# Two sliding-attention/FFN layers on one core: the order of the first layer norms, and one more tile's statistics on ScalarE

## Chip, cores, metric

One core of a Trainium2 chip. The metric is the device time of one execution in microseconds (us), as the median of the runs. A core has five engines that run side by side and meet through semaphores: PE (TensorE: matmuls and transposes into PSUM), DVE (VectorE), ACT (ScalarE), POOL (GpSimd) and SP (SyncE, which here only issues DMAs).

## What is computed

The input x has 2048 tokens of 1024 features in bf16. Two layers are applied, each of an attention block and a feed-forward block, with the same weights in both layers:

```python
x = x + A(layernorm(x), wqkv, wo)      # sliding attention, 32 heads of 32
x = x + B(layernorm(x), w1, b1, w2, b2) # 1024 -> 3584, gelu, -> 1024
# A: q, k, v = x @ wqkv; each position looks at 8 positions, 2 apart, at and before its own:
#    softmax over the 8 logits, weighted sum of v, then @ wo
# layernorm: (x - mean) / sqrt(var + 1e-5), no scale or offset
```

## The kernel before

All of x stays on the chip as 16 tiles `x[0]` to `x[15]` of 128 tokens. Four tiles make a group of 512 tokens; layer by layer and group by group the work items are n = 0 to 7. An item goes through `gen_qkv` (queries, keys and values in 8 chunks each, a chunk being 8 matmuls of 512 columns over the 8 slices k of the features), the attention proper on DVE (products of queries and keys, softmax, products with the values), `gen_wo` (output projection), `gen_ffn1` and `gen_ffn2`. Weights are loaded again for every item in tiles `wt` of 1 MB or 896 KB, in five buffers. PSUM is used as eight accumulators `acc` in rotation. The driver at the end of the program interleaves these parts: `stage` runs one of them unit by unit and calls `sides` at stated units, so attention on DVE for one item goes on beside PE's matmuls for another.

The wrapper `InOrder` records each engine's instructions. While its `on` is set, every instruction is tied to stand behind the last one of that engine in program order; `hold` makes everything later stand behind the last one. Where neither is set, the compiler's scheduler chooses. At the start of the program DVE, ACT, POOL and SP are all in order, and so is PE always.

**The start (`ln_first`, `queries_of_raw`).** PE can't wait until the first group is normalised. For tiles 0 and 1 it transposes the raw x (the function `transpose_on_pe`, two PSUM banks; ACT copies the banks to `raw` in two parts, the first two slices and then the other six, `copy_transposed`). Matmuls of seven query chunks c run over the raw x, slice by slice: `row(c, k)` for k = 0 to 7. Mean and inverse standard deviation enter afterwards: they are transposed on PE into rows (`spread_stats`, at (k, c) = (2, 6)), and `finish(c)` applies them, one DVE and one POOL instruction per chunk. Tiles 2 and 3 are normalised on DVE (`rest`) and transposed on PE within the same loop, at (5, 3) and (7, 6), both into the tile `bank`, which ACT copies to `xnT`. The eighth chunk follows in one piece (`row(7, k)`, `finish(7)`).

For keys and values the normalised tiles 0 and 1 are needed too. DVE writes them to `xn01`, and SP transposes them by DMA to `xnT` (list `first_early`). The order in which SP issues is:

```python
for xn, out in first_early:                        # two transposing DMAs, tiles 0 and 1
    sp.dma_start_transpose(out, xn.rearrange("s (k p) -> s k p", p=P))
wk = load_qkv(1, lambda: load_x(1, 2, 3))          # key weights: half, x[6], half
load_x(1, 3, 4)                                    # x[7]
load_x(2)                                          # x[8] to x[11]
early_tiles = ln_early((1, None), (2, qk_next))
```

**The next two groups (`ln_early`, `ln_stats_ahead`, `ln_end`).** The eight tiles of groups 1 and 2 are normalised during item 0. A tile takes two `bn_stats` (half a tile each) and a `bn_aggr` on DVE, a square root on ACT, a reciprocal and a `tensor_scalar` (the normalisation) on DVE, and a transposing DMA from SP. `ln_early` does tiles 4 to 9 one after the other, with the statistics of the next tile ahead of the normalisation of this one; it is a generator, and after its first step `last()`, which is `finish(7)`, is called. After the second step SP issues the loads of the value weights `wv`. For tiles 10 and 11 `ln_stats_ahead` takes the sums on ACT instead (Identity and Square, each with an accumulated sum) and mean and inverse root on POOL, at unit 9 of the stage; `ln_end` normalises and transposes them at unit 11.

In the lines of the profile, L92 is the line in `InOrder` through which every instruction of DVE, ACT, POOL and SP passes, L117 is the matmul helper `mm`, L230 the transposes of `transpose_on_pe`, L293 those of `spread_stats`. So groups are told apart by the names of their tiles: `stats`, `mvs` and `stds` are the layer norm's, `big` is a pool of three large buffers used for products and for normalised tiles, `vT` in the first 16 us is `raw`.

Of the kernel before, what the change touches and what calls it, by code (L numbers as in the profile page):

```python
# [8 lines left out]
ACT = mybir.ActivationFunctionType  # L9
# [8 lines left out]
def kernel(  # L18
# [18 lines left out]
    P = 128  # L37
# [195 lines left out]
    def copy_transposed(out, bank, parts):  # L233
        pst = bank[:].bitcast(BF16).rearrange("p (k t) -> p k t", t=P)
        for k0, k1 in zip(parts[:-1], parts[1:]):
            act.copy(out[:, k0:k1, :], pst[:, k0:k1, :])
# [11 lines left out]
    def ln_first():  # L248

        xnT = xa[0] = new_xnT()  # L250
        vec.on = act.on = True
        raw = attp.tile([P, KD, NT + 2], BF16, name="vT", bufs=2)
        vec.memset(raw[:, :, NT:NT + 2], 1.0)
        mv = lnp.tile([P, 4, 2], F32, name="mvs", bufs=1)
        std = lnp.tile([P, 4], F32, name="stds", bufs=1)
        rstd = lnp.tile([P, 4], F32, name="rstds", bufs=1)
        less = lnp.tile([P, 2], F32, name="lesses", bufs=1)

        def stats(tt):
            st6 = lnp.tile([P, 2, 6], F32, name="stats")  # L260
            for h in range(2):
                vec.bn_stats(st6[:, h, :], x[tt][:, h * HALF:(h + 1) * HALF])
            vec.bn_aggr(mv[:, tt, :], st6[:])

        def root(tt):
            act.activation(std[:, tt:tt + 1], mv[:, tt, 1:2], ACT.Sqrt, bias=eps_t[:])

        def norm(tt, out):
            if tt > 1:
                vec.reciprocal(rstd[:, tt:tt + 1], std[:, tt:tt + 1])  # L270
            vec.tensor_scalar(out=out, in0=x[tt][:], scalar1=mv[:, tt, 0:1], scalar2=rstd[:, tt:tt + 1],
                              op0=ALU.subtract, op1=ALU.mult)
            return out

        warm_ps = acc_tile()
        warm_up(7, warm_ps)
        banks = [acc_tile(), acc_tile()]
        for tt in range(2):
            transpose_on_pe(x[tt], raw[:, :, tt * P:(tt + 1) * P], banks[tt], (0, 2))
        warm_up(2, warm_ps)  # L280
        stats(0)
        root(0)
        copy_transposed(raw[:, :, 0:P], banks[0], (2, KD))
        stats(1)
        root(1)
        copy_transposed(raw[:, :, P:NT], banks[1], (2, KD))
        vec.tensor_scalar(out=less[:], in0=mv[:, 0:2, 0], scalar1=-1.0, scalar2=None, op0=ALU.mult)
        vec.reciprocal(rstd[:, 0:2], std[:, 0:2])
        by_token = iop.tile([P, 4, P], F32, name="tmp")

        def spread_stats(bank):
            for i, column in enumerate((less[:, 0:1], less[:, 1:2], rstd[:, 0:1], rstd[:, 1:2])):
                pe(nc.tensor.transpose(bank[:, i * P:(i + 1) * P], column.to_broadcast([P, P]), identf[:]))  # L293
            rows = by_token[:].rearrange("p i t -> p (i t)")
            act.copy(rows, bank[:])
            return rows[:, 0:NT], rows[:, NT:2 * NT]

        xn01 = bigp.tile([P, 2, D], BF16, name="big")
        first_early.append((norm(0, xn01[:, 0, :]), xnT[:, 0, :, :]))

        def rest():
            for tt in range(2, 4):
                stats(tt)
                root(tt)
                if tt == 2:
                    first_early.append((norm(1, xn01[:, 1, :]), xnT[:, 1, :, :]))
                xn = lnp.tile([P, D], BF16, name="xn", bufs=3)
                norm(tt, xn[:])
                first_late.append((xn, xnT[:, tt, :, :]))

        return raw, spread_stats, rest

    def queries_of_raw(wq, qT):
        raw, spread_stats, rest = st.pop("raw")
        first = {}

        def row(c, k):
            if k == 0:
                first[c] = acc_tile()
            mm(first[c][:, 0:NT + 2], lhsT=wq[k // (KD // 2)][:, k % (KD // 2), c::NCH], rhs=raw[:, k, :],  # L320
               start=(k == 0), stop=(k == KD - 1), skip_group_check=True)

        part = attp.tile([P, NCH, NT], F32, name="abc")

        def finish(c):
            vec.scalar_tensor_tensor(out=part[:, c, :], in0=less, scalar=first[c][:, NT:NT + 1], in1=first[c][:, 0:NT],
                                     op0=ALU.mult, op1=ALU.add)
            pool.tensor_tensor(out=qT[:, c, 0:NT], in0=part[:, c, :], in1=rstd, op=ALU.mult)

        for k in range(KD):  # L330
            for c in range(7):
                row(c, k)
                if (k, c) == (0, 6):
                    bank = acc_tile()
                if (k, c) == (2, 6):
                    less, rstd = spread_stats(bank)
                    rest()
                if (k, c) == (5, 3):
                    transpose_on_pe(*first_late.pop(0), bank)
                if (k, c) == (7, 6):  # L340
                    transpose_on_pe(*first_late.pop(0), bank, (0, KD // 2, KD))
        act.on = False
        act.hold()
        for c in range(7):
            finish(c)
        for k in range(KD):
            row(7, k)
        vec.on = False
        return lambda: finish(7)
# [41 lines left out]
    def gen_qkv(n, defer=False, qk_pool=None, v_late=False, qk_next=None, v_first=False, mix=0):  # L391
# [29 lines left out]
        if n == 0:  # L421
            last = queries_of_raw(wq, qT)
            for xn, out in first_early:
                sp.dma_start_transpose(out, xn.rearrange("s (k p) -> s k p", p=P))
            wk = load_qkv(1, lambda: load_x(1, 2, 3))
            load_x(1, 3, 4)
            load_x(2)
            early_tiles = ln_early((1, None), (2, qk_next))
            for tt in range(2):
                next(early_tiles)  # L430
                if tt == 0:
                    last()
            wv = load_qkv(2)
            for _ in early_tiles:
                pass
            vec.hold()
            sp.on = False
            sp.hold()
# [212 lines left out]
    def ln_early(*groups):  # L651

        tiles = []
        for n, pool in groups:
            xa[n] = new_xnT(pool)
            xns = bigp.tile([P, NTT, D], BF16, name="big") if pool is None else pool.tile([P, NTT, D], BF16, name="qT")
            for tt in range(NTT):
                xn = lnp.tile([P, D], BF16, name="xn", bufs=3)[:] if pool is None and tt > 1 else xns[:, tt, :]
                tiles.append((n * NTT + tt, xn, xa[n][:, tt, :, :]))
        vec.on = True  # L660
        ahead = ln_stats(tiles[0][0], root=True)
        on_act = tiles[-2:]
        tiles = tiles[:-2]
        for i, (t, xn, xT) in enumerate(tiles):
            mv_rstd = ahead
            if i + 1 < len(tiles):
                ahead = ln_stats(tiles[i + 1][0], root=True)
            vec.reciprocal(mv_rstd[1][:], mv_rstd[1][:])
            ln_norm(t, *mv_rstd, xn)
            sp.dma_start_transpose(xT, xn.rearrange("s (k p) -> s k p", p=P))  # L670
            if i + 1 == len(tiles):
                vec.on = False
            yield
        ln_rest.append(on_act)

    ln_rest = []

    def ln_end():
        vec.on = True
        for tt, (t, xn, xT) in zip((NTT - 2, NTT - 1), ln_rest.pop()):  # L680
            ln_norm(t, mv_ahead[:, tt, :], rstd_ahead[:, tt, :], xn)
            sp.dma_start_transpose(xT, xn.rearrange("s (k p) -> s k p", p=P))
        vec.on = False
# [27 lines left out]
    with tc.tile_pool(name="early", bufs=1) as early:  # L711
        sp.on = True
        load_x(1, 0, 2)
        stage(gen_qkv(0, qk_next=early), sides=at(9, ln_stats_ahead, 2, NTT - 2) + at(14, pool.dma_start, mask[0::NTT, :, :], first[:]) + at(11, ln_end) + at(14, load_b2))
        q1 = gen_qkv(1, defer=True, qk_pool=early, mix=NCH // 2)
        stage(q1, sides=at(0, gather, 0) + at(11, between, 0, 1) + at(11, hold) + each(av, 0, 12, 1))
        q2 = gen_qkv(2, defer=True)
        stage(q2, 18, sides=each(lambda n, q: load_b1(q), 2, 4, 4, 0, 4))
        hold()
        stage(gen_wo(0))  # L720
        hold()
        stage(q2, sides=at(0, new_prod, 1, 3, False) + at(0, add_prods, 1) + each(new_prod, 1, 0, 1, 4, 8))
        gather(1)
# [51 lines left out]
```

## Time and profile before

| | |
|---|---|
| median of 4 runs | 1229.05 us (1229.0 to 1229.18) |
| profiled execution | 1229.15 us, of which the span of the instructions is 1227.4 us |
| TensorE clock granted | 1.0 |
| busy in the span | PE 1222.7, DVE 865.8, ACT 314.8, POOL 121.7 us |
| DMA | 227 MB, mean 185 GB/s; from 16 to 22 us 394 GB/s |

A line of a timeline reads: start, length, engine, line of the program, operation, output<-input with shapes, count, and in brackets the idle time before it with what ended that. Neighbouring instructions of one kind are merged into one line. "SPq" is SP's instruction that issues a DMA; its length is the issuing, not the transfer. A line of waits reads: who waited for whom, us in total, times, longest. A line of DMA issues ends with KB each and the us from issue to landing. A group of instructions ends with the count, the busy time, the mean of one in ns and the idle time before.

### The profile page before, as it was taken

How to read it: one execution, taken by the hardware profiler on the slowest of the kernel's cores; microseconds unless marked ns; L12 is line 12 of the kernel's file. 1: busy time of each engine (PE TensorE's matmuls, PEld its weight loads, DVE VectorE, ACT ScalarE, POOL GpSimd, SP SyncE). 2: the span in 40 equal slices, each digit the busy share in tenths (PEclk: the TensorE clock that was granted, in tenths of full speed). 3: DMA queues.
4: the chain of work that ended last, by engine and by line, in shares of the span. 5: the costliest groups of instructions: out<-in, count | busy, mean ns of one | idle time of the engine just before them, and what ended most of it. 6: DMA issues, size and time to landing. Idle time of an engine off the chain costs nothing.

```text
span 1227.4 us, 14025 instructions
## 1 busy us (share of the span) xinstructions
PE 1222.7 (100%) x5769; PEld 632.1 (52%) x5769; DVE 865.8 (71%) x926; ACT 314.8 (26%) x498; POOL 121.7 (10%) x217
## 2 busy tenths in 40 slices
PE   9999999999999999999999999999999999999998
PEld 7666544456444554446544465444654444444444
DVE  7999897998997999375993759937598797011001
ACT  4443253014410244102431024310234001300310
POOL 2430006010101101100001000000000001000000
PEclk9999999999999999999999999999999999999999
DMA  9976665765738645856557565586664558446441
GB/s 312 263 233 181 182 201 170 202 186 191 226 120 257 183 151 162 237 172 172 168 158 223 172 171 187 153 217 199 171 204 148 186 191 211 149 160 193 158 135 51
DMA packets 225824, 227.18 MB, mean 185 GB/s; under 512 B 74000, under 2 KB 192928, under 8 KB 223712
## 3 DMA queue, kind: packets, MB, share of 16 engines
q1 hardware_dynamic: 216304, 208.17, 56.3%
q0 software_dynamic: 8880, 17.07, 4.3%
q8 instruction: 45, 0.74, 0.3%
q10 hardware_dynamic: 576, 1.05, 0.2%
q14 instruction: 19, 0.16, 0.0%
HBM read 189.01 MB, written 4.19 MB: 157 GB/s over the span
## 4 chain that ended last, share of the span: by engine, by line
PE 99%; DMA 0%; DVE 0%; ACT 0%; issue 0%
PE acc L117 99%; DMA x<-in_A_x_dram 0%; DVE stats L92 0%; PE acc L230 0%; ACT vT L92 0%; PE acc L293 0%; DVE mvs L92 0%; DVE x L92 0%; ACT stds L92 0%
## 5 line engine op out<-in xcount | busy, mean ns | idle before, releaser
L117 PE MATMUL acc<-xnT,wt 128*128 128x512 bf16 (+1 forms) x3328 | 712.9, 377 | 0.0
L117 PEld LDWEIGHTS <-wt 128*128 128x128 bf16 x3392 | 400.7, 119 | 318.8 <-issue 0.9
L117 PE MATMUL acc<-wt,hT 128*128 128x512 bf16 (+1 forms) x1820 | 388.1, 376 | 0.0
L117 PEld LDWEIGHTS <-hT 128*128 128x128 bf16 x1820 | 178.1, 98 | 209.0
L92 DVE TENSOR_TENSOR big<-big 128x2048 bf16<-128x2048 bf16 (+2 forms) x185 | 244.9, 1352 | 2.2
L92 ACT ACTIVATE hT<-acc,b1T 128x512 bf16<-128x512 f32 x224 | 151.7, 689 | 322.9 <-PE acc L117 322.8
L92 DVE TENSOR_TENSOR big<-qT,kT 128x4096 bf16<-128x4096 bf16 x64 | 143.8, 2283 | 37.7 <-ACT kT L92 35.9
L92 DVE TENSOR_TENSOR big<-abc,vT 128x4096 bf16<-128x4096 bf16 x64 | 144.6, 2283 | 8.3 <-DMA abc<-a 6.6
L92 DVE TENSOR_TENSOR tmp<-acc,b2bc 128x512 f32<-128x512 f32 x56 | 38.6, 689 | 156.1 <-PE acc L117 153.0
L92 ACT CAST qT<-acc 128x512 bf16<-128x512 f32 (+1 forms) x64 | 35.5, 558 | 278.1 <-PE acc L117 276.7
L117 PE MATMUL acc<-wt,oT 128*128 128x512 bf16 x448 | 97.9, 379 | 0.0
L92 DVE BATCH_NORM_STATS2 stats<-x 128x6 f32<-128x512 bf16 x116 | 77.3, 680 | 4.9 <-DMA x<-in_A_x_dram 3.8
L117 PEld LDWEIGHTS <-oT 128*128 128x128 bf16 x448 | 43.9, 98 | 52.9 <-issue 0.2
L92 DVE TENSOR_TENSOR x<-acc,big 128x512 bf16<-128x512 f32 (+1 forms) x9 | 5.7, 632 | 90.0 <-PE acc L117 90.0
L92 POOL TENSOR_TENSOR rstd<-mv,eps_t 128x1 f32<-128x1 f32 x48 | 14.6, 305 | 499.8 <-DVE mv L92 499.8
L92 ACT CAST vT<-acc 128x512 bf16<-128x512 f32 x64 | 37.5, 586 | 100.8 <-PE acc L117 100.8
L92 ACT CAST kT<-acc 128x512 bf16<-128x512 f32 x64 | 37.1, 585 | 59.6 <-PE acc L117 59.6
L92 DVE TENSOR_TENSOR x<-acc,x 128x512 bf16<-128x512 f32 x64 | 43.0, 671 | 5.8 <-PE acc L117 5.4
L92 DVE TENSOR_SCALAR xn<-x,mv,rstd 128x1024 bf16<-128x1024 bf16 x48 | 26.2, 545 | 19.9 <-POOL rstd L92 19.9
L92 DVE TENSOR_TENSOR x<-tmp,x 128x512 bf16<-128x512 f32 x56 | 38.6, 689 | 1.4
L92 POOL DMA_DIRECT2D big<-big x24 | 13.3, 564 | 212.2 <-DVE big L92 212.2
L92 ACT ACT_TABLE_LOAD x17 | 21.8, 1283 | 41.2 <-DVE e L92 28.2
(82 smaller groups left out, 303.8 us busy)
## 6 DMA issues: line engine op xcount, KB each, us to landing
wt<-in_B_w_dram SPq DMA_DIRECT2D x56, 1024.0 KB, 5.6
wt<-in_B_w_dram SPq DMA_DIRECT2D x64, 896.0 KB, 4.9
wt<-in_A_wqkv_dram SPq DMA_DIRECT2D x46, 1024.0 KB, 5.7
wt<-in_A_wo_dram SPq DMA_DIRECT2D x16, 1024.0 KB, 5.3
abc<-a POOLq DMA_DIRECT2D x32, 256.0 KB, 4.4
big<-big POOLq DMA_DIRECT2D x24, 256.0 KB, 3.9
out_dram<-x SPq DMA_DIRECT2D x31, 128.0 KB, 1.8
x<-in_A_x_dram SPq DMA_DIRECT2D x14, 256.0 KB, 5.9
```

What stands on the lines that cost most here:

```text
L92: inst = f(*args, **kwargs)
L117: return pe(nc.tensor.matmul(*args, **kwargs))
```

## The change

- In `ln_first` ACT copies the rest of both banks directly behind each other; the square roots of tiles 0 and 1 become one instruction behind them.
- DVE no longer normalises tile 0 ahead of the statistics of tile 2, nor tile 1 between tiles 2 and 3. `rest` now does: statistics of 2 and 3, normalisation of 2 and 3, then of 0 and 1.
- The transposes of tile 2 on PE move from (5, 3) to (6, 6).
- `ln_early` takes its tiles in two blocks, 4 and 5, then 6, 7 and 8: the statistics of the block, one square root for the whole block, and then its reciprocals, normalisations and transposing DMAs. `last()` and the load of the value weights keep their places in the code, between the generator's steps; a step now ends behind the statistics of a block.
- Tile 9 goes the way of tiles 10 and 11: sums on ACT, the rest on POOL, normalisation in `ln_end`.

```diff
-        def root(tt):
-            act.activation(std[:, tt:tt + 1], mv[:, tt, 1:2], ACT.Sqrt, bias=eps_t[:])
+        def root(t0, t1):
+            act.activation(std[:, t0:t1], mv[:, t0:t1, 1], ACT.Sqrt, bias=eps_t[:])
...
-        stats(0)
-        root(0)
-        copy_transposed(raw[:, :, 0:P], banks[0], (2, KD))
-        stats(1)
-        root(1)
-        copy_transposed(raw[:, :, P:NT], banks[1], (2, KD))
+        for tt in range(2):
+            copy_transposed(raw[:, :, tt * P:(tt + 1) * P], banks[tt], (2, KD))
+            stats(tt)
+        root(0, 2)
...
-        first_early.append((norm(0, xn01[:, 0, :]), xnT[:, 0, :, :]))
         def rest():
             for tt in range(2, 4):
                 stats(tt)
-                root(tt)
-                if tt == 2:
-                    first_early.append((norm(1, xn01[:, 1, :]), xnT[:, 1, :, :]))
+                root(tt, tt + 1)
+            for tt in range(2, 4):
                 xn = lnp.tile([P, D], BF16, name="xn", bufs=3)
                 norm(tt, xn[:])
                 first_late.append((xn, xnT[:, tt, :, :]))
+            for tt in range(2):
+                first_early.append((norm(tt, xn01[:, tt, :]), xnT[:, tt, :, :]))
...
-                if (k, c) == (5, 3):
+                if (k, c) == (6, 6):
                     transpose_on_pe(*first_late.pop(0), bank)
...
-            for tt in range(2):
-                next(early_tiles)
-                if tt == 0:
-                    last()
+            next(early_tiles)
+            last()
+            next(early_tiles)
...
-        ahead = ln_stats(tiles[0][0], root=True)
-        on_act = tiles[-2:]
-        tiles = tiles[:-2]
-        for i, (t, xn, xT) in enumerate(tiles):
-            mv_rstd = ahead
-            if i + 1 < len(tiles):
-                ahead = ln_stats(tiles[i + 1][0], root=True)
-            vec.reciprocal(mv_rstd[1][:], mv_rstd[1][:])
-            ln_norm(t, *mv_rstd, xn)
-            sp.dma_start_transpose(xT, xn.rearrange("s (k p) -> s k p", p=P))
-            if i + 1 == len(tiles):
-                vec.on = False
-            yield
+        on_act = tiles[-3:]
+        for t0, t1 in ((0, 2), (2, len(tiles) - 3)):
+            size = t1 - t0
+            mv = lnp.tile([P, 3, 2], F32, name="mv3")
+            std = lnp.tile([P, 3], F32, name="std3")
+            for i in range(size):
+                stats = lnp.tile([P, 2, 6], F32, name="stats")
+                for h in range(2):
+                    vec.bn_stats(stats[:, h, :], x[tiles[t0 + i][0]][:, h * HALF:(h + 1) * HALF])
+                vec.bn_aggr(mv[:, i, :], stats[:])
+            act.activation(std[:, 0:size], mv[:, 0:size, 1], ACT.Sqrt, bias=eps_t[:])
+            yield
+            for i in range(size):
+                t, xn, xT = tiles[t0 + i]
+                vec.reciprocal(std[:, i:i + 1], std[:, i:i + 1])
+                ln_norm(t, mv[:, i, :], std[:, i:i + 1], xn)
+                sp.dma_start_transpose(xT, xn.rearrange("s (k p) -> s k p", p=P))
+        vec.on = False
...
-        for tt, (t, xn, xT) in zip((NTT - 2, NTT - 1), ln_rest.pop()):
+        for tt, (t, xn, xT) in zip(range(1, NTT), ln_rest.pop()):
...
-        stage(gen_qkv(0, qk_next=early), sides=at(9, ln_stats_ahead, 2, NTT - 2) + ...
+        stage(gen_qkv(0, qk_next=early), sides=at(9, ln_stats_ahead, 2, 1) + ...
```

More of the change, by code (lines that the diff above doesn't have):

```diff
@@ L713 @@
         load_x(1, 0, 2)
-        stage(gen_qkv(0, qk_next=early), sides=at(9, ln_stats_ahead, 2, NTT - 2) + at(14, pool.dma_start, mask[0::NTT, :, :], first[:]) + at(11, ln_end) + at(14, load_b2))
+        stage(gen_qkv(0, qk_next=early), sides=at(9, ln_stats_ahead, 2, 1) + at(14, pool.dma_start, mask[0::NTT, :, :], first[:]) + at(11, ln_end) + at(14, load_b2))
         q1 = gen_qkv(1, defer=True, qk_pool=early, mix=NCH // 2)
```

## The prediction

> **What bounds the kernel now.** I read, in this order: the page's busy times and chain, the waits of PE, the timelines of PE, SP, DVE and ACT in the first 50 us (in windows small enough to show single instructions), and the landings of single loads. All times are us from the span's start. T0 to T11 are the transposes (on PE or by DMA) of x tiles 0 to 11; wk0 and wk1 are the two 1 MB halves of the first key weights.
>
> ```profile
> PE 1222.7 (100%) x5769; PEld 632.1 (52%) x5769; DVE 865.8 (71%) x926; ACT 314.8 (26%) x498; POOL 121.7 (10%) x217
> PE 99%; DMA 0%; DVE 0%; ACT 0%; issue 0%
> ```
> ```profile
> PE acc L117 <- DVE vT L92: 1.0, 1, 1.0
> PE acc L117 <- ACT vT L92: 0.3, 1, 0.3
> ```
> PE is the bound: it is busy in 1222.7 of 1227.4 us, and these two are all its waits. The first is the very start; the second is at 8.12, where row k=2 of the first queries waits for a PSUM copy.
>
> ```profile
> L117 PE MATMUL acc<-xnT,wt 128*128 128x512 bf16 x463 | 100.1, 379 | 0.0
> ```
> This group of PE (window 15.2 to 122) shows the pace: 100.1/463 = 216 ns for each 512-column matmul, with no idle time. So the change can only gain in the first 15 us, and it loses what PE is made to wait later. A "busy" PE hides short stalls, so I took starts: from 7.54 to 8.12 is 0.58 where neighbours are 0.11 apart, 0.47 lost; about 0.2 is lost before 6.77 and 0.17 before 13.80. At most 0.85 us is to be had.
>
> ```profile
> 8.65 4.09 SPq L92 DMA_TRANSPOSE xnT<-big  x2
> 12.80 0.57 SPq L92 DMA_DIRECT2D wt<-in_A_wqkv_dram  x1
> 13.42 0.50 SPq L92 DMA_DIRECT2D x<-in_A_x_dram  x1
> 13.96 0.43 SPq L92 DMA_DIRECT2D wt<-in_A_wqkv_dram  x1
> 14.44 3.47 SPq L92 DMA_DIRECT2D x<-in_A_x_dram  x5
> ```
> This is SP's timeline. One in-order queue issues T0 and T1 (at 8.65 and 10.11, each behind its DVE normalisation), then wk0 at 12.80, x6, wk1 at 13.96, x7 to x11.
>
> ```profile
> wt<-in_A_wqkv_dram SPq DMA_DIRECT2D x1, 1024.0 KB, 8.3
> ```
> Asked for the issue at 13.96 alone, the DMA view gives 8.3 to landing (8.25 in the trace): wk1 is there at 22.22. Key chunk 0 starts on PE at 22.14, and its fifth matmul, the first that reads wk1, at 23.00. **Margin: 0.79 us.** That number decides.
>
> **What the Trainium skill says.** "DMA: Bandwidth & Descriptors", Queues, rings and completion order: each DMA engine takes the descriptors of a ring in order. The trace agrees: T1 lands at 16.28, wk0 18.84, x6 19.48, wk1 22.22, in order of issue; a late queue head makes all behind it late. "TensorE: Matmul & The Clock Gate", Part 1: 215.7 ns per warm 512-column matmul (216 here), and half clock after an idle window of about 3.4 us; no run here shows what a gap of 2 us does. "GPSIMD Engine Reference", Key points: GpSimd shares its SBUF interfaces with VectorE. The trace agrees: the same one-column TENSOR_SCALAR takes 0.23 at 28.44, and 1.97 at 30.08 beside DVE's products.
>
> **The change, part by part.**
>
> *Copies ahead of the roots (ACT).* The root at 5.74 leaves and the big copy of bank 0 takes its place: 5.74 to 6.52 instead of 5.93 to 6.72. Bank 1's copy follows at 6.42 to 7.20, instead of behind the second root, 7.29 to 8.07. The one root for both columns still waits for the mean and variance of tile 1 (7.05), so it runs at 7.10 (0.30) and the reciprocal stays at 7.43. PE starts row 2 at about 7.46 instead of 8.12: 0.66 gained. Row k=4's weights (landing 9.51) then hold PE up for 0.1.
>
> *Transposes of tile 2 on PE at (6,6) instead of (5,3).* They come at 11.86 to 12.31. T3 uses the same bank at (7,6), behind ACT's copy of it (0.99 long). Before, 17 matmuls lay between; now 7, 0.77 us. The copy runs 12.51 to 13.50, so T3 starts at 13.55 and not at 13.08: a new stall of 0.47. T3 began at 13.80 before, so 0.25 is left of the gain; queries start at 14.91 instead of 15.16, key chunk 0's fifth matmul is wanted at 22.76.
>
> *The order on DVE.*
> ```profile
> 8.08 1.28 DVE L92 BATCH_NORM_STATS2 stats<-x 128x6 f32<-128x512 bf16 x2
> 9.39 0.21 DVE L92 BATCH_NORM_AGGREGATE mvs<-stats 128x2 f32<-128x12 f32 x1
> 10.54 0.55 DVE L92 TENSOR_SCALAR xn<-x,mvs,rstds 128x1024 bf16<-128x1024 bf16 x1
> ```
> In DVE's timeline a tile's statistics take 1.44 start to start (two of these, then the aggregate), a normalisation 0.46 to 0.55, a reciprocal 0.16. New order from 7.60: statistics of 2 (x2 lands at 7.81) and 3, to 10.79; reciprocal and norm 2 to 11.46; 3 to 12.13; norm 0 to 12.59; norm 1 to 13.05. The seven `finish` start at 12.97 instead of 13.54. So norm 0 ends at 12.59 where it ended at 8.16.
>
> *What stands behind it on SP.* T0 waits for norm 0, and wk0, x6, wk1, x7 to x11, T4, T5 and the value weights stand behind T0 and T1. T0 can be issued at 12.68. What two transposes cost SP depends on the DMA rings: 1.35 + 2.64 at 8.65, behind loads still running (T1's issue ends as the last load lands, 12.92), but
>
> ```profile
> 35.12 2.64 SPq L92 DMA_TRANSPOSE xnT<-qT  x2
> ```
> 1.26 and 1.29 here. At 12.68 the loads are out (x5 lands at 12.92), so I take 2 x 1.3: wk0 is issued at 15.29, **2.49 later**. The other end is 4.05 for the two, wk0 at 16.7.
>
> *Sum.* wk1 landed 9.42 after wk0's issue; the query weights at 37.85 and 38.48, with nothing ahead of them, land 5.76 and 8.60 after the first issue, and with x6 between (0.65 from one x landing to the next) that is 9.25. So wk1 is there at 24.54 to 24.71. PE wants it at 22.76: a **stall of 1.8 to 2.0** in the middle of key chunk 0, and PE goes on at 24.6 to 24.75 instead of 23.00. Net +1.6 to +1.75, I take **+1.7**. The front gain does not enter: PE waits for wk1 whenever it arrives. wk0 (21.1) is in time for 21.9.
>
> *Downstream.* The value weights' second half landed at 35.29 and is wanted at 36.81; with both shifted (+2.5 and +1.7), 0.7 is left. The second key half of group 1 goes from 49.79 to some 52.6 (three transposes ahead of it now), landing 58.4, wanted at 59.2.
>
> *Tile 9's statistics on ScalarE.* DVE loses 1.28 + 0.21 (1.44 in its pace), and its norm moves to `ln_end`. ACT gains Identity 1.06, Square 1.13 and two reads of 0.19, some 2.4 us between key casts; PE has eight accumulators of 1.73 each to run ahead in, so I cost it at nothing. POOL gains three one-column operations of about 2.1 beside DVE's products; tile 11's inverse root goes from 41.4 to some 47.5, about when DVE reaches the norms (45.6 before): up to 1.0 of DVE waiting. DVE also waits for x6, x7, x8, each 2.5 late, so its products start at about 30.6 instead of 29.72, and after three norms it is 1.4 to 2.4 late.
>
> ```profile
> DVE big L92 <- DMA abc<-a: 1.4, 1, 1.4
> DVE stats L92 <- DMA x<-in_A_x_dram: 0.6, 1, 0.6
> ```
> These are all of DVE's named waits from 14 to 124: it runs without slack of its own to the last attention output at 122.15, which PE wants at 123.80 (chunk 7 of the output projection from 122.29). That margin of 1.65, plus PE's own 1.7, covers 1.4 to 2.4. The large groups after that (FFN, projections) are unchanged.
>
> **The rivals.**
> 1. *Slower by more:* T0 and T1 keep the 4.0 of their old place on SP. Against it: the rings are empty at 12.7. It gives +1.7 + 1.4 = +3.1, 1232.2. It decides from 3.2 us of shift on: 3.2 - 0.79 = 2.46, which is 0.2% of 1229.05 and about what a measurement of this kernel can tell from no change. Two other ways lead there: DVE over 3.3 late at 122, or a clock halved by the gap (at most some 3.4 us at half pace, an estimate from the page above: +1.7).
> 2. *Weights in time:* the DMA stream before was half idle from 12 to 15 (212 GB/s in 12 to 16, 394 after), so an issue 2.5 later might cost under 0.8. Against it: the 5.8 us from issue to landing start only at issue, at 37.85 too. It gives -0.25 at the least, 1228.8, up to 0.66 if T3's stall is absent.
> 3. *The ScalarE part alone is felt:* DVE gets slack, but PE waits for DVE nowhere from 15 to 122. 0 either way, and it adds to none of the above.
>
> **How the numbers follow.** Profiled execution before: 1227.4 span + 1.75 around it = 1229.15; after, 1229.1 + 1.75 = 1230.85; the median of the runs is 0.10 below the profiled time: **1230.7**. Chances: forecast (+1.0 to +2.46) 0.60, slower rival and its kin 0.29, in time or nearly (-0.7 to +1.0) 0.10, something unseen that gains 0.01. Low end 1229.4 takes part of rival 2 in, high end 1232.7 most of rival 1. Faster by over 0.2% needs 2.46 us, more than the 0.85 there is.
>
> **What would show it.** Right: SP's first DMA_TRANSPOSE near 12.7, the next load near 15.3; PE with one wait of about 1.9 near 22.8 on the DMA of wt; the wait of 0.3 at 8.1 gone; T3 held by ACT's copy at 13.5; nothing at 122. Wrong: wk0 issued before 13.6 (no stall), or PE waiting for DVE at the projection, for the value weights near 38, or at half pace after the gap.

## The result and the profile after

The changed kernel takes 1231.11 us (median of 35 runs, 1230.44 to 1233.33) against 1229.13 of the kernel before (53 runs, 1228.80 to 1229.85): a ratio of 1.0018 (95% interval 1.0014 to 1.0023), 2.0 us slower. The profiled execution took 1231.05 us, of which the span is 1229.2 us: 1.8 us more than the span before.

The page's busy times, and what PE waited for:

```profile
PE 1223.2 (100%) x5769; PEld 633.2 (52%) x5769; DVE 864.8 (70%) x922; ACT 316.0 (26%) x497; POOL 127.5 (10%) x220
```
```profile
PE acc L117 <- DMA wt<-in_A_wqkv_dram: 1.6, 1, 1.6
PE acc L117 <- DVE vT L92: 1.0, 1, 1.0
PE acc L230 <- DVE abc L92: 0.3, 1, 0.3
```
PE's busy time rises by only 0.5 us. Of the two waits before, the wait of 0.3 for ScalarE's copy at 8.12 is gone, and two waits are new: one for weights, and one of 0.3 in front of a transpose. PE's timeline shows where the first is:

```profile
22.46 0.81 PE L117 MATMUL acc<-xnT,wt 128*128 128x512 bf16 x3
24.91 0.65 PE L117 MATMUL acc<-xnT,wt 128*128 128x512 bf16 x2 [1.63 <-DMA wt<-in_A_wqkv_dram]
```
Key chunk 0 does the four matmuls of wk0, the last at 22.90, and goes on with wk1 at 24.91. (Start to start this is 2.01 where 0.216 is the pace: 1.80 lost. The view says 1.63, since it counts from the modelled end of the last matmul.) The fifth matmul stood at 23.00 before, so PE is 1.90 later here; it is 1.96 later from the sixth matmul on and 1.91 later from the first output projection (123.2 before) to the end. SP's timeline says why wk1 is late:

```profile
12.64 2.87 SPq L92 DMA_TRANSPOSE xnT<-big  x2
15.56 0.57 SPq L92 DMA_DIRECT2D wt<-in_A_wqkv_dram  x1
16.19 0.50 SPq L92 DMA_DIRECT2D x<-in_A_x_dram  x1
16.73 0.43 SPq L92 DMA_DIRECT2D wt<-in_A_wqkv_dram  x1
17.20 3.35 SPq L92 DMA_DIRECT2D x<-in_A_x_dram  x5
```
T0 and T1 are issued at 12.64 instead of 8.65, wk0 at 15.56 instead of 12.80 and wk1 at 16.73 instead of 13.96; wk1 lands at 24.86. SP itself was idle from 8.20 to 12.64, with the next loads standing behind T0. What T0 waits for is in DVE's timeline:

```profile
7.91 0.17 DVE L92 RECIPROCAL rstds<-stds 128x2 f32<-128x2 f32 x1 [0.93 <-ACT stds L92]
7.99 1.26 DVE L92 BATCH_NORM_STATS2 stats<-x 128x6 f32<-128x512 bf16 x2
9.41 1.23 DVE L92 BATCH_NORM_STATS2 stats<-x 128x6 f32<-128x512 bf16 x2
...
12.07 1.00 DVE L92 TENSOR_SCALAR big<-x,mvs,rstds 128x1024 bf16<-128x1024 bf16 x2
12.98 2.86 DVE L92 SCALAR_TENSOR_TENSOR abc<-tmp,acc 128x256 f32<-128x256 f32 x7
```
Both normalisations into `xn01` (the `big` at 12.07) now stand behind the statistics and normalisations of tiles 2 and 3. No instruction on DVE became slower; they became later.

A smaller part of the delay lies ahead of that. Before, DVE waited 0.16 for the root of tile 1:

```profile
7.42 0.17 DVE L92 RECIPROCAL rstds<-stds 128x2 f32<-128x2 f32 x1 [0.16 <-ACT stds L92]
```
Now it waits 0.93 for the one root of both tiles, since on ScalarE that root stands behind the big copies:

```profile
5.90 1.78 ACT L92 COPY vT<-acc 128x256 bf16<-128x256 bf16 x3 [0.48 <-PE acc L230]
7.55 0.32 ACT L92 ACTIVATE stds<-mvs,eps_t 128x2 f32<-128x2 f32 x1
```
The copies in turn wait for PE's transposes of tiles 0 and 1, which in this execution started 0.107 apart up to 5.55 (0.056 in the one before). So DVE began the statistics of tile 2 at 7.99, though x2 had landed at 7.59: some 0.4 of T0's delay, an estimate from these two times.

### The profile page after: what moved, and what is told of

It is laid out like the page before. It is cut to its first block, busy times and chain, and to the rows that moved or that the text cites. A ratio compares the mean times of both kernels' runs of the same rounds, so it can differ in the third digit from the quotient of the medians.

```text
span 1229.2 us, 14025 instructions
## 1 busy us (share of the span) xinstructions
PE 1223.2 (100%) x5769; PEld 633.2 (52%) x5769; DVE 864.8 (70%) x922; ACT 316.0 (26%) x497; POOL 127.5 (10%) x220
## 4 chain that ended last, share of the span: by engine, by line
PE 98%; DMA 1%; DVE 1%; ACT 0%; SPq 0%; issue 0%
PE acc L117 98%; DMA wt<-in_A_wqkv_dram 1%; DVE abc L92 0%; DVE stats L92 0%; ACT vT L92 0%; PE acc L230 0%; SPq L92 0%; DVE xn L92 0%; DVE big L92 0%; DVE x L92 0%; DVE mvs L92 0%; DVE rstds L92 0%; ACT stds L92 0%; DVE vT L92 0%
## 5 line engine op out<-in xcount | busy, mean ns | idle before, releaser
L92 POOL DMA_DIRECT2D big<-big x24 | 13.3, 564 | 212.2 <-DVE big L92 212.2
```

Source lines behind the costliest of these rows:

```text
L92: inst = f(*args, **kwargs)
```

## The experiments

The theory (A in the expectations) was that the whole loss is the late issue of the key weights behind T0 and T1 on SP. The rivals: B, that the stall at the PSUM bank or the new order on DVE and ScalarE is felt; C, that when the weights are moved the transposes become what is late. Measured times are medians unless the text says otherwise; the kernel before, run beside each on the same chip, took 1229.12 to 1229.15.

**The key weights ahead of the transposes.**

```diff
+            wk = load_qkv(1, lambda: load_x(1, 2, 3))
             for xn, out in first_early:
                 sp.dma_start_transpose(out, xn.rearrange("s (k p) -> s k p", p=P))
-            wk = load_qkv(1, lambda: load_x(1, 2, 3))
```


> The changed kernel, with the key weights (wk0, x6, wk1) issued on SP ahead of the two transposing DMAs of tiles 0 and 1 instead of behind them. Theory A (the whole loss is the key weights' late issue behind those transposes): wk0 is issued near 8.5 instead of 15.56, wk1 lands before 19, T1 lands near 20 to 21, still ahead of key chunk 0 at 22.2; PE has no wait there, and the time falls by 1.8 to 2.2 to 1228.8 to 1229.3. Rival B (the loss comes from the stall of tile 3's transposes at the PSUM bank, or from DVE's and ScalarE's new order): still 1230.5 to 1231.2. Rival C (the transposes take the weights' place as what is late): PE waits for the DMA of xnT near 22 instead, 1229.5 to 1231.

Measured: 1229.41 (ratio 1.0003, 0.9995 to 1.0011). SP's timeline:

```profile
8.36 0.46 SPq L92 DMA_DIRECT2D wt<-in_A_wqkv_dram  x1
9.16 0.33 SPq L92 DMA_DIRECT2D x<-in_A_x_dram  x1
9.54 0.43 SPq L92 DMA_DIRECT2D wt<-in_A_wqkv_dram  x1
12.55 7.36 SPq L92 DMA_TRANSPOSE xnT<-big  x2
```
wk0 is issued at 8.36 and wk1 lands at 20.11; PE has no wait for weights. T0 is as late as in the changed kernel, so the place of the weights behind it on SP carries the loss. It is no gain either: T1 landed at 21.98, with PE at key chunk 0 at 22.17. Rival C is close, though this execution shows no such wait.

**The normalisations of tiles 0 and 1 in their old places**, the rest of the change kept.

```diff
+        first_early.append((norm(0, xn01[:, 0, :]), xnT[:, 0, :, :]))
...
                 root(tt, tt + 1)
+                if tt == 2:
+                    first_early.append((norm(1, xn01[:, 1, :]), xnT[:, 1, :, :]))
...
-            for tt in range(2):
-                first_early.append((norm(tt, xn01[:, tt, :]), xnT[:, tt, :, :]))
```


> The changed kernel, with the normalisations of tiles 0 and 1 back in their old places on DVE (tile 0 ahead of the statistics of tile 2, tile 1 ahead of the normalisation of tile 2). All else of the change stays: copies, one root, (6, 6), the blocks, tile 9 on ScalarE. Theory A: T0 is issued near 8.6 and wk0 near 12.8 as before the change, wk1 lands near 22.2 and PE does not wait: 1228.7 to 1229.2. Rival B (bank stall, DVE blocks, ScalarE): 1230.5 to 1231.2, unchanged.

Measured: 1229.31 (1.0002, 0.9994 to 1.0010). SP's timeline:

```profile
8.60 4.59 SPq L92 DMA_TRANSPOSE xnT<-big  x2
13.24 0.57 SPq L92 DMA_DIRECT2D wt<-in_A_wqkv_dram  x1
```
wk0 at 13.24 is 0.44 later than before the change, wk1 lands at 22.70, and PE wants it at 23.07: 0.37 to spare. Copies, single root, (6, 6), the blocks and tile 9 on ScalarE are all still in, and the stall at the PSUM bank is too, 0.49 at 13.3. They are not the 2 us. Whether they cost nothing is not shown: this median and the one of the run before lie 0.19 and 0.29 above the kernel before, each 0.1 above the expected range. The intervals take in no difference, and where the rest would come from is open. In the last version below, which has no such stall, nothing is left (1229.14 beside 1229.15).

**The transposes of tile 2 back at (5, 3).**

```diff
-                if (k, c) == (6, 6):
+                if (k, c) == (5, 3):
```


> The changed kernel, with the PE transposes of tile 2 back at (5, 3). Theory A: the bank stall of 0.48 near 13.4 goes, and PE waits about 0.5 for tile 2's normalisation at (5, 3) or not; either way it still waits for wk1 until 24.9, so the time stays within 0.3 of the changed kernel, 1230.9 to 1231.3. Rival B (the bank stall is part of the loss): 0.4 to 0.5 less, 1230.6.

Measured: 1231.39 (1.0022, 1.0013 to 1.0031; 10 runs), 0.1 above the expected range; the profiled execution 1230.69. The bank stall goes, and tile 2 waits 0.60 at 10.57 for its normalisation. PE comes to the keys 0.4 earlier than in the changed kernel, and waits until wk1 is there, at 24.48. Where PE stands just before the wait does not matter.

The profiled time alone would fit rival B (1230.6), but it has another cause: wk1 lands 0.38 earlier because T0 is issued at 12.25 instead of 12.64, and that begins ahead of anything that this experiment moved.

```profile
6.88 0.30 ACT L92 ACTIVATE stds<-mvs,eps_t 128x2 f32<-128x2 f32 x1
7.58 1.29 DVE L92 BATCH_NORM_STATS2 stats<-x 128x6 f32<-128x512 bf16 x2 [0.20 <-DMA x<-in_A_x_dram]
```
In this execution PE's transposes sped up at 4.2 (0.056 apart from there), the root came at 6.88, and DVE began right behind the landing of x2 (7.55). So the pace of PE's first transposes does reach the time, through the copies that the change put ahead of the root.

**One more transposing DMA ahead of the weights.**

```diff
-            for xn, out in first_early:
+            for xn, out in first_early + first_early[1:]:
```


> The changed kernel, with the transposing DMA of tile 1 issued twice: one more DMA_TRANSPOSE on SP ahead of the key weights. Theory A: each one costs SP 1.25 to 1.5, so wk0 is issued near 16.9, wk1 lands near 26.2, PE's wait grows by 1.25 to 1.5 and the time to 1232.3 to 1232.7; if a gap of 3.2 us halves the clock afterwards, up to 1.7 more. Rival B: no change, 1231.1.

Measured: 1235.89 (1.0059, 1.0047 to 1.0072). More than expected, for two reasons. The repeat writes the same output as T1, so it was issued only when T1 had landed (17.29): wk0 came at 18.64, 3.08 later and not 1.25 to 1.5, and wk1 landed at 28.43. And the clock fell. In the view of stretches (busy us with counts for PE, PEld, DVE, ACT and POOL, then the granted PE clock, DMA share, GB/s):

```profile
22.00:24.50 2.50, 0.15 (x2) 0.00 (x0) 0.00 (x0) 0.37 (x1) 0.00 (x0) 1.00 1.02 371
24.50:31.30 6.80, 4.75 (x11) 1.73 (x12) 3.63 (x8) 0.58 (x1) 0.00 (x0) 0.50 1.16 359
31.30:36.00 4.70, 4.70 (x23) 3.06 (x22) 3.09 (x9) 2.36 (x5) 0.00 (x0) 0.99 1.02 235
```
PE stood still from 22.1 to 25.1, and for 6.8 us after 24.5 it had half its clock: 11 matmuls there, 427 ns apart, against 216. From 28.47 to 31.3 that cost 1.4 us.

**One part alone: the normalisations of tiles 0 and 1 last, in the kernel before.**

```diff
-        first_early.append((norm(0, xn01[:, 0, :]), xnT[:, 0, :, :]))
...
-                if tt == 2:
-                    first_early.append((norm(1, xn01[:, 1, :]), xnT[:, 1, :, :]))
...
+            for tt in range(2):
+                first_early.append((norm(tt, xn01[:, tt, :]), xnT[:, tt, :, :]))
```


> The kernel before, with one part of the change alone: the normalisations of tiles 0 and 1 on DVE behind those of tiles 2 and 3. Copies, roots, (5, 3), the blocks and tile 9 stay as before. Theory A: T0 is issued near 12.6, wk0 near 15.5, wk1 lands near 24.8, PE waits until then: the whole loss of the change, 1230.9 to 1231.3. Rival B (bank stall at (7, 6), DVE blocks, ScalarE): no loss, 1229.0 to 1229.4.

Measured: 1232.62 (1.0030, 1.0018 to 1.0041; 6 runs): all of the loss and 1.5 us more, against an expected 1230.9 to 1231.3. DVE's timeline, which differs from the change here:

```profile
10.22 0.17 DVE L92 RECIPROCAL rstds<-stds 128x1 f32<-128x1 f32 x1 [0.81 <-ACT stds L92]
12.77 0.16 DVE L92 RECIPROCAL rstds<-stds 128x1 f32<-128x1 f32 x1 [0.36 <-ACT stds L92]
13.43 1.00 DVE L92 TENSOR_SCALAR big<-x,mvs,rstds 128x1024 bf16<-128x1024 bf16 x2
```
With each tile finished before the next tile's statistics, DVE idles for each root. The two normalisations start at 13.43, 1.36 later than in the changed kernel, and T0 at 14.00. wk1 lands at 25.86 and PE goes on 2.90 later than before (a wait of 0.58 for DVE at 14.3 lies ahead of that and adds nothing); a second wait for key weights (0.58 at 60.3, those of group 1, behind the longer SP queue) makes it 3.5. So the block order of statistics in the change is worth over a microsecond, once the normalisations of 0 and 1 are last; the loss is having them last.

**The other part alone: tile 9's statistics on ScalarE, in the kernel before.**

```diff
-        on_act = tiles[-2:]
-        tiles = tiles[:-2]
+        on_act = tiles[-3:]
+        tiles = tiles[:-3]
...
-        for tt, (t, xn, xT) in zip((NTT - 2, NTT - 1), ln_rest.pop()):
+        for tt, (t, xn, xT) in zip(range(1, NTT), ln_rest.pop()):
...
-        stage(gen_qkv(0, qk_next=early), sides=at(9, ln_stats_ahead, 2, NTT - 2) + ...
+        stage(gen_qkv(0, qk_next=early), sides=at(9, ln_stats_ahead, 2, 1) + ...
```


> The kernel before, with one part of the change alone: tile 9's sums on ScalarE, the rest on GpSimd, its normalisation in ln_end. Theory A: PE waits for neither, so no difference, 1229.0 to 1229.3; DVE ends its attention outputs some 0.5 to 1.4 earlier or later than 122.15 and PE does not show it. Rival B (DVE or ScalarE is felt): more than 0.3 either way.

Measured: 1229.08 (1.0000, 0.9992 to 1.0008). DVE starts its products at 27.39 instead of 29.72, waits for GpSimd once,

```profile
44.70 0.56 DVE L92 TENSOR_SCALAR qT<-x,mv_ahead,rstd_ahead 128x1024 bf16<-128x1024 bf16 x1 [0.46 <-POOL rstd_ahead L92]
```
and ends its last attention output at 121.85 instead of 122.15. PE, whose only wait in that run is the one at the very start, does not show it.

**A small dose: x7 ahead of the weights.**

```diff
+            load_x(1, 3, 4)
             wk = load_qkv(1, lambda: load_x(1, 2, 3))
-            load_x(1, 3, 4)
             load_x(2)
```


> The changed kernel with the load of x7 put ahead of the key weights, behind T0 and T1: a small dose. Theory A: wk0 is issued about 0.45 to 0.6 later and wk1's data comes 0.65 later, so PE's wait grows by 0.5 to 0.7 and the typical time is 1231.6 to 1231.8. Executions some 2 us longer should be more frequent than in the changed kernel (6 of 35), if they are those in which the longer gap halves PE's clock; if the gap has nothing to do with them, they stay as rare. Rival B: no change, 1231.1.

Measured: 1231.96 (1.0026, 1.0015 to 1.0038; 7 runs), and the profiled execution likewise, 0.16 above the expected range. wk1 lands at 25.72, 0.86 later than in the changed kernel (SP had issued T0 0.1 later as well), and the time rises by 0.85. Two of the seven executions were granted a mean clock under 1; from 6 of 35 that is too few to tell apart.

**The next dose: x7 and x8 ahead**, edited in the same way.

> The changed kernel with x7 and x8 put ahead of the key weights, behind T0 and T1: the next dose after x7 alone. Theory A: wk1 lands 0.65 later again, near 26.3, PE's wait is near 3.1, and without a lower clock the time is 1232.5 to 1232.7. If a gap of this length halves PE's clock in some executions, those take 1.4 to 2 us more, and they should be half or more of all; otherwise all lie within 0.5 of each other.

Measured: 1234.60 (1.0046, 1.0032 to 1.0060; 5 runs, 1234.26 to 1236.02). wk1 lands at 26.81. In the profiled execution, 1236.02, PE had half its clock from 26.1 to 32.9:

```profile
26.10:32.90 6.80, 6.04 (x15) 2.39 (x16) 6.25 (x13) 1.55 (x4) 0.00 (x0) 0.50 1.08 291
```
From 26.86 on that costs 3.0 us. All five executions were granted a mean clock under 1.

**Two tries for a faster kernel**, both from the changed kernel with both key halves ahead of T0 and T1 and x6 behind them. The first also has DVE in the order statistics 2, norm 2, statistics 3, norm 3, norm 0, norm 1, and tile 2's transposes at (5, 5).

> A try for a faster version, from the changed kernel: both halves of the key weights ahead of T0 and T1 on SP, x6 behind them, DVE in the order statistics 2, norm 2, statistics 3, norm 3, norm 0, norm 1, and the PE transposes of tile 2 at (5, 5). Theory A: no wait for weights; tile 2 is ready near 10.9 where PE comes near 11.0, tile 3 near 13.4 where PE comes near 13.1: queries start 0.2 to 0.5 earlier than in the kernel before. T1 lands near 20, ahead of key chunk 0. 1228.6 to 1229.0, if the saving is not lost to T1 landing after 21.8. Rival C (the transposes are now what is late): PE waits for the DMA of xnT near 22, 1229.1 to 1229.8.

Measured: 1229.70 (1.0005, 0.9996 to 1.0013). A miss, and by the cause that the run with the norms last alone had shown: DVE idles for the roots, so `finish(0)` comes late and with it the accumulator of the eighth chunk.

```profile
15.06 1.06 PE L117 MATMUL acc<-vT,wt 128*128 128x258 bf16 x8 [0.59 <-DVE abc L92]
```
The second keeps the change's own order on DVE, with tile 2's transposes at (6, 3).

> A second try for a faster version, from the changed kernel: both halves of the key weights ahead of T0 and T1 on SP, x6 behind them (DVE in the change's own order), and the PE transposes of tile 2 at (6, 3), so that ten matmuls instead of seven lie between them and tile 3's. Theory A: wk1 lands near 19.5, T1 near 21.4; tile 2 waits 0.1 to 0.2 for its normalisation, tile 3 no longer for the bank; queries start 0.2 to 0.4 earlier than in the kernel before where the clock rises early, and T1 is just in time: 1228.7 to 1229.1. If T1 is then what PE waits for, 1229.1 to 1229.5.

Measured: 1229.14 beside 1229.15 (1.0000, 0.9992 to 1.0008). The profiled execution is among the quickest of all, 1228.73: its queries start at 14.73 instead of 15.16, with ten matmuls between the two groups of transposes,

```profile
11.67 0.61 PE L230 MATMUL acc<-ident,xn 128*128 128x128 bf16 x8
12.12 1.27 PE L117 MATMUL acc<-vT,wt 128*128 128x258 bf16 x10
13.38 0.61 PE L230 MATMUL acc<-ident,xn 128*128 128x128 bf16 x8
```
and no wait for T1, which landed at 21.23. The median of 13 runs shows no gain. No version beats the kernel before by more than the runs scatter.

**All together.** Take PE's own demand for wk1 in the kernel before (23.00, so a landing of 22.96) and its profiled time, 1229.15. Of each kernel this is the one execution that was profiled:

| kernel | wk1 lands | 1229.15 + (landing - 22.96) | profiled time |
|---|---|---|---|
| keys first, tile 2 at (6, 3) | 19.40 | in time | 1228.73 |
| keys first, statistics in turn | 19.50 | in time; PE waits 0.59 for DVE instead | 1229.85 |
| keys first | 20.11 | in time | 1229.13 |
| tile 9 alone | 21.95 | in time | 1229.08 |
| old norm places | 22.70 | in time | 1229.15 |
| tile 2 at (5, 3) | 24.48 | 1230.67 | 1230.69 |
| the change | 24.86 | 1231.05 | 1231.05 |
| x7 ahead | 25.72 | 1231.91 | 1231.96 |
| norms last alone | 25.86 | 1232.05, + 0.58 second wait = 1232.63 | 1232.70 |
| x7, x8 ahead | 26.81 | 1233.00, + 3.0 clock = 1236.0 | 1236.02 |
| third transpose | 28.43 | 1234.62, + 1.4 clock = 1236.0 | 1235.89 |

Past the margin, each microsecond of delay of this one 1 MB load is a microsecond of the kernel.

## Why the prediction was right, point by point

- *What decides.* The margin of 0.79 us between wk1's landing and its first use was the right number: in the table nothing else enters until another wait or the clock does. The forecast was 1230.7, 1.65 above the kernel before; measured is 1231.11, 2.0 above. PE's resumption shifted by 1.90 against +1.7. The other 0.2 is that the median lies 0.06 above the profiled execution and was put 0.10 below it.
- *The term that was short* is the shift of wk0's issue: 2.76 (12.80 to 15.56) and not 2.49. The two transposes took SP 2.92 to wk0's issue and not 2.61: 1.52 for T0, 1.24 for T1, and the gaps between. "2 x 1.3" was near for T1 and low for T0. The rest, 9.30 from wk0's issue to wk1's landing, lay within the 9.25 to 9.42.
- *T0's time* was met within 0.05 (12.64 for 12.68), in part by luck. The root was put at 7.10 and the reciprocal at 7.43; they came at 7.55 and 7.91, because the copies ahead of the root ended at 7.68 and not at 7.20, behind PE's slow transposes. (With tile 9 alone, PE's transposes were as slow, but the roots stand in their old places, and the reciprocal came at 7.38.) Most of this was hidden, since the prediction had DVE wait for x2 anyway, at 7.81; in this execution x2 came at 7.59.
- *The front.* T3's new stall behind ScalarE's copy is there as worked out (0.48 for 0.47; ScalarE copies from 12.85 for 1.01). The view names "DVE abc" as the releaser; the copy ended at 13.86 and PE started at 13.91, and in four of the experiments with the same stall the view names the ScalarE copy. Of the gain of 0.66 at row 2, 0.21 is left in this execution (7.91 for 8.12): PE's pace doubled only at about 5.7, so the rows started at 6.33 and not at 5.89. Queries came at 15.26 instead of the 14.91 forecast. That did not matter, as the prediction said: PE waits for wk1 whenever it arrives. What the prediction did not see is that PE's slow start also moves wk1's arrival, as above.
- *Downstream* the bounds were too narrow for DVE. Products started at 30.83 (30.6 forecast), but the last attention output came at 124.84, 2.69 late and not 1.4 to 2.4. The DMA that spreads the attention weights (`abc<-a`) landed 4.70 after its last issue instead of 3.91, and DVE waited 2.2 for it instead of 1.4. PE wanted that output at 125.76, so 0.9 was left and nothing showed. Value weights and group 1's key weights came in time, as forecast.
- *The rivals.* The first (4.0 us for the two transposes) was wrong in size, 2.9. Its kin, the clock, happened after all: not in the typical execution, but in six of 35, and for longer than the 3.4 us that the prediction put as the most (6.8 in both traces that show it; up to 2.2 us above the median where +1.7 was the bound). The second (weights in time) failed on what had been put against it: wk0 took 5.92 from issue to landing, for 6.04 before. The third, that tile 9's part is not felt, holds: 1229.08 alone.
- *Two slips*, on which nothing hangs: 3.2 - 0.79 is 2.41, so rival 1 decides from a shift of 3.25 on; and the 0.85 us that could be had leaves out 0.19 at 5.89 (0.41 from the start before, where 0.22 is the pace).

## What to carry to other kernels

When an instruction is moved later, follow the DMA that waits for it, and then everything behind that DMA on its in-order queue: here a normalisation moved by 4.4 us on an engine with room held up a weight load that did not depend on it. Find the first use of each load behind it, and compare the slack (0.79 us) with the shift (2.76 us); a gain ahead of that point is lost as soon as the load is what PE waits for. Loads without a dependency belong ahead of issues that must wait, as long as what is moved behind them is still in time: here that took the loss away, and gained nothing over the kernel before. And when a small instruction is put behind a large one on the same engine, as the root behind the copies, ask who waits for the small one.

## What the runs showed of the hardware that was not expected

- **A gap of PE can have a second price.** In the changed kernel, six of 35 executions took 1232.77 to 1233.33, and these six alone were granted a mean clock of 0.998 or 0.999; the other 29, at a clock of 1.000, lie between 1230.44 and 1231.66. The gap in the profiled execution is about 1.8 us. In the other kernels, by the gap in the profiled execution of each: about 1.8 us (tile 2 at (5, 3)), 3 of 10; 2.3 us, 1 of 6; 2.5 us, 2 of 7; with two gaps of 1.1 and 2.5 us, four matmuls apart, or 3.1 and 1.9 us, 5 of 5 each. The gaps of the executions that were not profiled are not known. None of the 75 runs of the kernel before beside the experiments had a lower clock, nor any of the 65 of the five kernels without the gap. No such execution of the changed kernel was itself profiled; that its clock fell behind this gap is inferred from the two traces of longer gaps. In these the half clock begins at 24.5, 2.35 after PE had stopped (22.15), and at 26.1, 1.5 after PE had stopped for the second time (24.56). The Trainium skill ("TensorE: Matmul & The Clock Gate", Part 1) puts the fall of the clock behind an idle window of about 3.4 us; here it came after less, so the measurement decides: a gap shorter than that window is not safe. Why one execution has it and the next has not is open.
- The half-clock stretch was 6.8 us long in both traces that hold it.
- Of T0 and T1, issued when the last load ahead of them had landed or landed within 0.4 us, the first took SP 1.3 to 2.0 us and the second 1.23 to 1.27, in all six kernels with such a pair. With loads still on their way T1 took longer, and its issue ended 0.1 to 0.2 us before the last of them landed, in all six kernels of that kind: in the kernel before 2.64 (to 12.75; the last x landed at 12.92), in the run with the key weights first 4.4 (15.55 to 19.91; wk1 at 20.11).
